# A gated mix of a 2-D spectral filter and a dense block: half of the tiles of x transposed by DMA

## The chip, the cores and the metric

The kernel runs on one core of one Trainium2 chip. The metric is the device time of one execution in microseconds (us). A core has a matrix engine (PE, with its weight loads PEld), a vector engine (DVE), an activation engine (ACT), a general engine (POOL) and a sync engine (SP) that issues DMAs; 16 DMA engines carry what SP, ACT and POOL issue.

## What is computed

```python
def _A_ref(x, w_r, w_i):                      # x: (1, 2048, 512)
    X = jnp.fft.rfft2(x.astype(jnp.float32))
    X = X * (w_r + 1j * w_i)                  # (2048, 257)
    return jnp.fft.irfft2(X, s=(S, D)).astype(jnp.bfloat16)

def _B_ref(x, w1, b1, w2):                    # w1: (512, 1792), w2: (1792, 512)
    h = jnp.einsum("bsd,df->bsf", x, w1) + b1
    sp = jnp.log1p(jnp.exp(-jnp.abs(h))) + jnp.where(h > 0, h, 0)
    return jnp.einsum("bsf,fd->bsd", h * jnp.tanh(sp), w2)

x = A_x
g = sigmoid((x * gate_w).sum(-1, keepdims=True))
return g * _A_ref(x, A_w_r, A_w_i) + (1 - g) * _B_ref(x, B_w1, B_b1, B_w2)
```

All inputs and the output are bfloat16. Both branches read the same x.

## The kernel before

The 2048 rows of x are 16 tiles of 128 rows by 512 columns; row 16 p + t of x is partition p of tile t, in `xo`. Both branches want x with its columns on the partitions, in `xT`. A tile gets there by four PE transposes of 128x128 into a PSUM bank (`tr{t}`, L522), which also sort the rows by an index `bx`, and one eviction by DVE or ACT (`evx{t}`, L451 or L452). All use bank 1, apart from tiles 1 to 3.

**Spectral branch.** It is a chain of small Fourier matrices. For each pair of tiles DVE makes four sums and differences (`ty`, `tz`, `t0`, `t2`, L537); for each tile PE does `a1` (L551 to L554, all in bank 0) and an eviction `e1` follows; for each four tiles PE does `s1` (L572, banks 2 to 5), four evictions `e2` bring it to `Ybuf`, and two DMAs `r1w` write it to `scr1`, a scratch in DRAM. When all of `scr1` is written, four DMAs `r1r` read it back in another order into `Abuf`. Then come four rounds of `s2` on PE (L689), the products with the filter W on DVE (L699), sums on POOL or DVE (L705), `s2i` (L732) and `r2w`, the trip through a second scratch, and at the end for each tile `s1i` (L764), `a1i` (L776), a scaling by the gate (L781) and two adds (L784).

**Dense branch.** Four chunks `c` of four tiles. `mm1` (L810) is 14 groups of four matmuls for a chunk, each followed by the activation on ACT (L819); `mm2` (L851) multiplies with w2 in two halves of seven matmuls for a tile. It has no latency of its own and stands between the steps of the spectral branch on PE.

**Gate.** `gdot` (L594, DVE) forms the dot products from `xo` once the third `s1` is placed; two small DMAs `gdj` on SP's queue sort them by `bx`; a sigmoid gives `gcol`.

**Order.** `_Graph.schedule` (L223) makes the order of every engine's work when the kernel is built. It takes the task that can start first by written-down durations, and among those within 0.1 us of it the one of the highest priority; a task of several possible engines goes where it ends first. For DMAs it keeps two clocks: `dq_free` for those issued by SP and ACT, `dq2_free` for POOL's, each with a written-down rate `bw` (POOL's with a factor 1.5). On the chip each engine then runs its list strictly in order and waits at an instruction until what it depends on is done.

**Loads.** SP's queue, in this order: x tile 0, tiles 1 to 3, w1 in pieces, the constants FD, tiles 4 to 7, M1's first half, w1, tiles 8 to 11, the last piece of w1 (`t_w1`), tiles 12 to 15, M1's second half, sm, gw, gd. POOL's queue: b1, then W in four DMAs and w2 in two, all of which wait for `t_w1`:

```python
        ld_x(8, 12)
        t_w1 = ld_w1(3)
        ld_x(12, 16)
        ...
                           writes=[("W", i, h)], nbytes=64 * 8224, queue="pool", deps=[t_w1])
```

W is first read by `wcols` on POOL (L609), whose result goes into two small matmuls `rcw` (L629, L630). All DMAs are issued at one line, L421.

Of the kernel before, what the change touches and what calls it, by code (L numbers as in the profile page):

```python
# [7 lines left out]
BF = mybir.dt.bfloat16  # L8
# [5 lines left out]
NT = 16  # L14
# [308 lines left out]
def _build(nc, A_x, A_w_r, A_w_i, B_x, B_w1, B_b1, B_w2, gate_w, out):  # L323
# [11 lines left out]
    with es:  # L335
        def sb(name, shape, dt):
            return es.enter_context(nc.sbuf_tensor(name, shape, dt))

        xo = sb("xo", [128, NT, 512], BF)
        xT = sb("xT", [128, 4, NT, 128], BF)  # L340
        Tg = sb("Tg", [128, 8192], BF)
        yb = sb("yb", [128, 2, 2, 256], BF)
        act = sb("act", [128, 3, NFT, 512], BF)
# [54 lines left out]
        psb = ps.bitcast(BF)  # L398

        xv = A_x[0].rearrange("(p t) d -> p t d", t=16)  # L400
        ov = out[0].rearrange("(a b t) d -> b a t d", b=2, t=16)
        w1v = B_w1.rearrange("(dt p) f -> p dt f", p=128)
        w2v = B_w2.rearrange("(ft p) n -> p ft n", p=128)
# [10 lines left out]
        out_sem = new_sem("s_out")  # L414
        n_out_dma = [0]

        def dma(name, dst, src, reads=(), writes=(), nbytes=0, deps=(), is_out=False, prio=None, queue="sp", bw=300e3):
            dur = 1.0 if queue == "pool" else 0.5

            def fn(e, _dst=dst, _src=src):  # L420
                return e.dma_start(_dst, _src)  # L421

            t = G.add(name, queue, dur, fn, reads=reads, writes=writes, lat=2.0 + nbytes / bw, deps=deps, prio=prio)
            t.xfer = nbytes / bw
            t.isdma = True
            if is_out:
                t.sem = out_sem
                n_out_dma[0] += 1
                t.semval = 16 * n_out_dma[0]
            else:  # L430
                t.sem = new_sem("d_" + name)
                t.semval = 16
            return t

        def mm(n):
            return n / 2400.0 + 0.0025
# [28 lines left out]
        def ld_x(t0, t1):  # L465
            dma(f"ld_x{t0}", xo[:, t0:t1, :], xv[:, t0:t1, :], writes=[("x", t) for t in range(t0, t1)], nbytes=128 * 1024 * (t1 - t0),
                bw=260e3 if t0 < 4 else 380e3)

        W1S = [(0, 2), (2, 6), (6, 10), (10, 14)]

        def ld_w1(i):
# [14 lines left out]
        ld_x(4, 8)  # L486
        ld_m1(0)
        ld_w1(2)
        ld_x(8, 12)
        t_w1 = ld_w1(3)  # L490
        ld_x(12, 16)
        ld_m1(1)
        dma("ld_sm", sm[:], d_SM[:], writes=["sm"], nbytes=128 * 1280)
        dma("ld_gw", gwb[:, :], gate_w.unsqueeze(0).to_broadcast([128, 512]), writes=["gw"], nbytes=128 * 1024)
# [1 line left out]
        for i in range(2):  # L496
            for h in range(2):
                dma(f"ld_W{i}{h}", WT[64 * h:64 * h + 64, i, :, :].rearrange("p g k -> p (g k)"), Wv[i][h],
                           writes=[("W", i, h)], nbytes=64 * 8224, queue="pool", deps=[t_w1])
        WALL = [("W", i, h) for i in range(2) for h in range(2)]  # L500
        for h in range(2):
            dma(f"ld_w2_{h}", w2_sb[:, 7 * h:7 * (h + 1), :], w2v[:, 7 * h:7 * (h + 1), :],
                writes=[("w2", h)], nbytes=128 * 7 * 1024, queue="pool", deps=[t_w1])


        G.add("zero", "dve", 0.15, lambda e: e.memset(zt[:, :], 0.0), writes=["zt"], prio=99.0)
# [7 lines left out]
        s1_tasks = []  # L514
        t_r1w = []
        for t in range(NT):
            tbk = 1 + t if 1 <= t < 4 else 1

            def f_tr(e, t=t, tbk=tbk):
                ins = None  # L520
                for dt_ in range(4):
                    ins = e.transpose(psb[:, tbk, 128 * dt_:128 * (dt_ + 1)], xo[:, t, 128 * dt_:128 * (dt_ + 1)], perm[:, :])  # L522
                return ins

            t_tr = pe(f"tr{t}", 4 * mm(128), f_tr, reads=[("x", t), "perm"], writes=[("bank", tbk)], prio=SP0 + 1.0)
            evict(f"evx{t}", 512, xT[:, :, t, :], psb[:, tbk, 0:512].rearrange("p (r j) -> p r j", r=4),
                  [("bank", tbk)], [("xT", t)], prio=SP0 + 1.0)
            if t == 3:
                pe("tr_small", 0.1, lambda e: e.transpose(psb[:, 0, 0:14], braw[0:14, :], id14[:, :]),
                   reads=["braw", "id14"], writes=[("bank", 0)], deps=[t_tr], prio=SP0 + 1.0)  # L530
                G.add("ev_small", "dve", 0.2, lambda e: e.tensor_copy(out=b1f[:, :], in_=psb[:, 0, 0:14]), reads=[("bank", 0)], writes=["b1f"], prio=SP0 + 1.0)

            if t % 2 == 1:
                t0, yi = t - 1, (t // 2) % 2

                def tt(name, o, i0, i1, op, n, reads, writes):
                    G.add(name, "dve", dve_dur(n, rate=2.0), lambda e: e.tensor_tensor(out=o, in0=i0, in1=i1, op=op),  # L537
                          reads=reads, writes=writes, prio=SP0 + 0.9)

                lo, hi = xT[:, 0:2, t0:t0 + 2, :], xT[:, 2:4, t0:t0 + 2, :]  # L540
                yy = yb[:, yi, :, :].rearrange("p r (t j) -> p r t j", t=2)
                xr = [("xT", t0), ("xT", t)]
                tt(f"ty{t}", yy, lo, hi, ALU.add, 512, xr, [("y", yi)])
                tt(f"tz{t}", Tb[:, 2:4, t0:t0 + 2, :], lo, hi, ALU.subtract, 512, xr, [("Tz", t0), ("Tz", t)])
                tt(f"t0{t}", Tb[:, 0, t0:t0 + 2, :], yy[:, 0], yy[:, 1], ALU.add, 256, [("y", yi)], [("T0", t0), ("T0", t)])
                tt(f"t2{t}", Tb[:, 1, t0:t0 + 2, :], yy[:, 0], yy[:, 1], ALU.subtract, 256, [("y", yi)], [("T2", t0), ("T2", t)])

        for t in range(NT):
            def f_a1(e, t=t):
                pr = ps[:, 0, :].rearrange("p (r x) -> p r x", r=4)  # L550
                e.matmul(pr[:, 0, :], Tb[:, 0, t, :], FDs[:, 0:128], start=True, stop=True)  # L551
                e.matmul(pr[:, 2, :], Tb[:, 1, t, :], FDs[:, 128:256], start=True, stop=True)
                for i in range(2):
                    ins = e.matmul(pr[:, 1::2, :], Tb[:, 2 + i, t, :], FDs[:, 256 + 256 * i:512 + 256 * i].rearrange("p (r x) -> p r x", r=2),  # L554
                                   start=(i == 0), stop=(i == 1))
                return ins

            pe(f"a1_{t}", 2 * mm(128) + 2 * mm(256), f_a1, reads=[("T0", t), ("T2", t), ("Tz", t), "FD"],
               writes=[("bank", 0)], prio=SP0)
            evict(f"e1_{t}", 512, In1[:, t, :].rearrange("p (c r q) -> p c r q", c=2, r=4),  # L560
                  ps[:, 0, :].rearrange("p (r c q) -> p c r q", r=4, c=2),
                  [("bank", 0)], [("In1", t)], prio=SP0 + 0.2)

            if t % 4 == 3:
                def f_s1(e, t0=t - 3):
                    ins = None
                    for tt_ in range(4):
                        tk = t0 + tt_
                        for c in range(2):
                            for bx in range(2):  # L570
                                r = slice(64 * bx, 64 * bx + 64)
                                ins = e.matmul(ps[:, 2 + 2 * (tt_ // 2) + bx, 256 * (tt_ % 2):256 * (tt_ % 2) + 256], M1s[r, tk, c, :],  # L572
                                               In1[r, tk, 256 * c:256 * c + 256], start=(c == 0), stop=(c == 1))
                    return ins

                B25 = [("bank", i) for i in range(2, 6)]
                s1_tasks.append(pe(f"s1_{t}", 8 * mm(256) + 0.19, f_s1, reads=[("In1", t - i) for i in range(4)] + [("m1", t // 8)], writes=B25, prio=SP0 + 0.4))
                for bx in range(2):
                    for i in range(2):
                        b0 = 16 * bx + t - 3 + 2 * i  # L580
                        evict(f"e2_{b0}", 512, Y1[:, b0:b0 + 2, :].rearrange("p b k -> p (b k)"), ps[:, 2 + 2 * i + bx, :],
                              [("bank", 2 + 2 * i + bx)], [("Y1", b0), ("Y1", b0 + 1)], prio=SP0 + 0.6)
            if t % 4 == 3:
                for bx in range(2):
                    b0 = 16 * bx + t - 3
                    t_r1w.append(dma(f"r1w{t}_{bx}", scr1_w[:, b0:b0 + 4, :], Y1[:, b0:b0 + 4, :],
                                     reads=[("Y1", b0 + i) for i in range(4)], writes=[("scr1", b0 + i) for i in range(4)],
                                     nbytes=128 * 4 * 512, prio=SP0 + 1.0))
# [211 lines left out]
        for c in range(NCH):  # L800
            hb = c % 3
            G.cur_prio = PR['mm1c0'] if c == 0 else PR['mm1c'] - c
            for ft in range(NFT):
# [3 lines left out]
                def f_mm1(e, c=c, ft=ft, bank=bank):  # L807
                    ins = None
                    for dt_ in range(4):
                        ins = e.matmul(ps[:, bank, :], w1_sb[:, dt_, 128 * ft:128 * (ft + 1)],  # L810
                                       xT[:, dt_, 4 * c:4 * c + 4, :], start=(dt_ == 0), stop=(dt_ == 3))
                    return ins

                t_mm1 = pe(f"mm1_{c}_{ft}", 4 * mm(512), f_mm1,
                   reads=[("xT", 4 * c + i) for i in range(4)] + [("w1", ft)], writes=[("bank", bank)])
                if c == 0 and ft == 0:
                    G.filled = t_mm1
                G.add(f"mish_{c}_{ft}", "act", act_dur(512, True),
# [162 lines left out]
```

## Time and profile before

| | us |
|---|---|
| median of 3 runs (lowest to highest) | 142.26 (142.17 to 143.02) |
| the profiled execution | 142.56 |
| its span, first to last instruction | 140.8 |
| PE busy | 136.2 |
| DVE busy | 86.3 |
| ACT busy | 81.4 |
| POOL busy | 31.9 |
| L522, the transposes: 64 matmuls, mean of one 0.242, busy | 6.7 |
| evictions of transposes: 10 on DVE of 0.424, 6 on ACT of 0.597 | |
| DMA moved 21.38 MB | |

Times inside an execution are counted from its first instruction. Busy time of PE is modelled and overlaps: a matmul of 512 columns shows 0.380 us, while in the chain of work four of them take 0.86 us. Of a DMA two things are shown: its issue on the queue of an engine, and the time from issue to landing; the packets of q1 are those of SP's queue, of q0 those of POOL's.

### The profile page before, as it was taken

To read this page: it belongs to the slowest core of one execution; us is meant where nothing else is said; L and a number is where in the kernel's file an instruction comes from. 1 tells how busy PE (TensorE), PEld (TensorE's weight loads), DVE (VectorE), ACT (ScalarE), POOL (GpSimd) and SP (SyncE) were. 2 spreads that over 40 slices of the span, in tenths; PEclk is the share of its full clock that TensorE was granted. 3 is DMA by queue.
4 is the path that set the end of the run, shared out by engine and by line. 5 is a ranking of instruction groups with operands and counts; after the bars stand their busy time and mean duration, and the time that the engine had idled before them with its cause. 6 is when DMAs were issued, how large, how long until landed. Compare 5 with 4: busy or idle time off the path is not lost.

```text
span 140.8 us, 2515 instructions
## 1 busy us (share of the span) xinstructions
PE 136.2 (97%) x946; PEld 74.2 (53%) x946; DVE 86.3 (61%) x192; ACT 81.4 (58%) x128; POOL 31.9 (23%) x62
## 2 busy tenths in 40 slices
PE   6999999999999999999999999999999999999991
PEld 4756656455544435435445444544444666766670
DVE  0276757748999303983983893592200499999831
ACT  4448797969874487488058437532411685776300
POOL 4000670003000001560440440340000144256400
PEclk9999999999999999999999999999999999999999
DMA  3999999999705485700300300300359615333422
GB/s 87 334 382 387 393 245 214 239 333 366 222 8 154 151 254 202 289 0 10 143 0 0 149 0 5 149 2 0 143 150 277 179 27 119 80 79 92 98 52 58
DMA packets 16556, 21.38 MB, mean 152 GB/s; under 512 B 1248, under 2 KB 12384, under 8 KB 16160
## 3 DMA queue, kind: packets, MB, share of 16 engines
q1 hardware_dynamic: 15552, 17.22, 39.3%
q0 software_dynamic: 832, 3.94, 10.4%
q8 instruction: 7, 0.11, 0.3%
q10 hardware_dynamic: 160, 0.07, 0.2%
q14 instruction: 5, 0.04, 0.1%
HBM read 14.92 MB, written 6.29 MB: 151 GB/s over the span
## 4 chain that ended last, share of the span: by engine, by line
PE 92%; ACT 4%; DVE 0%; issue 0%
PE ps L810 33%; PE ps L851 32%; PE ps L776 5%; PE ps L509 3%; PE ps L689 3%; PE ps L572 3%; PE ps L732 3%; PE ps L764 3%; PE ps L522 2%; ACT Ybuf L452 2%; PE ps L833 2%; PE ps L554 2%; ACT act L819 1%; PE ps L551 1%; ACT Abuf L452 1%; ACT xT L452 1%
## 5 line engine op out<-in xcount | busy, mean ns | idle before, releaser
L810 PE MATMUL ps<-xT,w_sb 128*128 128x512 bf16 x224 | 54.2, 380 | 0.4 <-ACT act L819 0.3
L819 ACT ACTIVATE act<-ps,b1f 128x512 bf16<-128x512 f32 x56 | 38.1, 690 | 21.8 <-PE ps L810 16.4
L851 PE MATMUL ps<-w_sb,act 128*128 128x512 bf16 x210 | 48.3, 379 | 0.0
L810 PEld LDWEIGHTS ps<-xT,w_sb 128*128 128x128 bf16 x224 | 20.0, 98 | 24.1 <-ACT act L819 5.7
L851 PEld LDWEIGHTS ps<-w_sb,act 128*128 128x128 bf16 x210 | 20.1, 98 | 22.4 <-issue 0.4
L699 DVE TENSOR_TENSOR misc<-ps,WT 128x512 f32<-128x512 f32 x32 | 19.9, 685 | 12.6 <-PE ps L689 12.6
L705 POOL TENSOR_TENSOR misc<-misc 128x255 bf16<-128x255 f32 x16 | 11.4, 731 | 41.0 <-DVE misc L699 41.0
L784 POOL TENSOR_TENSOR Tg<-misc 128x256 bf16<-128x256 f32 x12 | 10.3, 873 | 27.9 <-ACT misc L781 27.9
L790 ACT ACTIVATE xo<-ps,omg 128x512 bf16<-128x512 f32 x11 | 7.6, 687 | 15.2 <-PE ps L851 15.0
L451 DVE CAST Ybuf<-ps 128x512 bf16<-128x512 f32 (+1 forms) x10 | 8.8, 900 | 9.3 <-PE ps L732 8.2
L781 ACT ACTIVATE misc<-ps,gcol 128x512 f32<-128x512 f32 x16 | 10.3, 685 | 5.0 <-PE ps L776 4.0
L451 DVE CAST misc<-ps 128x512 bf16<-128x512 f32 x8 | 5.5, 683 | 11.4 <-PE ps L764 11.4
L784 DVE TENSOR_TENSOR Tg<-misc 128x256 bf16<-128x256 f32 x20 | 12.0, 629 | 0.7 <-ACT misc L781 0.7
L594 DVE SCALAR_TENSOR_TENSOR junk<-xo,gwb 128x512 bf16<-128x512 bf16 x16 | 11.0, 689 | 0.7
L452 ACT ACTIVATE Ybuf<-ps 128x512 bf16<-128x512 f32 (+1 forms) x14 | 9.4, 718 | 2.6 <-PE ps L572 1.6
L451 DVE COPY xT<-ps 128x512 bf16<-128x512 bf16 x10 | 4.2, 424 | 9.1 <-PE ps L522 9.0
L776 PE MATMUL ps<-GDs,misc 128*128 128x256 bf16 x64 | 9.3, 273 | 0.0
L452 ACT ACTIVATE Abuf<-ps 128x512 bf16<-128x512 f32 x12 | 7.2, 602 | 0.0
L776 PEld LDWEIGHTS ps<-GDs,misc 128*128 128x128 bf16 x64 | 6.0, 98 | 2.3
L522 PEld LDWEIGHTS ps<-pid,xo 128*128 128x128 bf16 x64 | 5.2, 110 | 3.0 <-issue 0.4
L522 PE MATMUL ps<-pid,xo 128*128 128x128 bf16 x64 | 6.7, 242 | 0.0
L705 DVE TENSOR_TENSOR misc<-misc 128x255 bf16<-128x255 f32 x16 | 6.4, 441 | 0.0
(81 smaller groups left out, 115.7 us busy)
## 6 DMA issues: line engine op xcount, KB each, us to landing
scr<-Ybuf SPq DMA_DIRECT2D x8, 256.0 KB, 9.3
Abuf<-scr SPq DMA_DIRECT2D x4, 512.0 KB, 4.5
scr<-Ybuf SPq DMA_DIRECT2D x4, 512.0 KB, 3.0
Abuf<-scr SPq DMA_DIRECT2D x8, 256.0 KB, 5.3
w_sb<-in_B_w_dram POOLq DMA_DIRECT2D x2, 896.0 KB, 17.5
out_dram<-xo SPq DMA_DIRECT2D x14, 128.0 KB, 2.3
w_sb<-in_B_w_dram SPq DMA_DIRECT2D x3, 512.0 KB, 7.9
xo<-in_A_x_dram SPq DMA_DIRECT2D x3, 512.0 KB, 8.7
```

The costliest lines, as they stand in the source:

```text
L451: G.add_multi(name, [("dve", dve_dur(n), lambda e: e.tensor_copy(out=dst, in_=src)), ("act", act_dur(n), lambda e: e.activation(dst, src, ...
L452: ("act", act_dur(n), lambda e: e.activation(dst, src, AF.Copy))],
L522: ins = e.transpose(psb[:, tbk, 128 * dt_:128 * (dt_ + 1)], xo[:, t, 128 * dt_:128 * (dt_ + 1)], perm[:, :])
L594: lambda e, t=t: e.scalar_tensor_tensor(out=junk[:, :], in0=xo[:, t, :], scalar=1.0, in1=gwb[:, :], op0=ALU.mult, op1=ALU.mult, accum_out= ...
L699: lambda e, Pb=Pb, Wu=Wu, bk=bk, pb=pb: e.tensor_tensor(out=Pb[:, pb, :].rearrange("p (c r q) -> p c r q", c=2, r=4), in0=ps[:, bk, :].rea ...
L705: fz = (lambda e, c=c, Pb=Pb, op=op, pb=pb, i=i, zb=zb: e.tensor_tensor(out=Zb[:, zb, i, c, 1:256], in0=Pb[:, pb, 1:256], in1=Pb[:, pb, 25 ...
L776: ins = e.matmul(ps[:, yk, 256 * (j // 2):256 * (j // 2) + 256], TT[:, ts_, j, :], GDs[:, j, :], start=(j % 2 == 0), stop=(j % 2 == 1))
L781: lambda e, t=t, gb=gb, yk=yk: e.activation(gEO[:, gb, :], ps[:, yk, :], AF.Copy, scale=gcol[:, t:t + 1]),
L784: fg = (lambda e, i=i, op=op, t=t, gb=gb: e.tensor_tensor(out=ga[:, t, 256 * i:256 * i + 256], in0=gEO[:, gb, 0:256], in1=gEO[:, gb, 256:5 ...
L810: ins = e.matmul(ps[:, bank, :], w1_sb[:, dt_, 128 * ft:128 * (ft + 1)], xT[:, dt_, 4 * c:4 * c + 4, :], start=(dt_ == 0), stop=(dt_ == 3))
L819: lambda e, ft=ft, bank=bank, hb=hb: e.activation(act[:, hb, ft, :], ps[:, bank, :], AF.Mish, bias=b1f[:, ft:ft + 1]),
L851: ins = e.matmul(ps[:, bank, :], act[:, hb, ft, 128 * tl:128 * (tl + 1)], w2_sb[:, ft, :], start=(ft == 0), stop=(ft == NFT - 1))
```

## The change

Tiles 8 to 15 of x are no longer transposed by PE. Four transposing DMAs (`ld_xt`, two for each four tiles, one for each `bx`) in SP's queue read them from DRAM into `xT` behind the last piece of w1. W and w2 no longer wait for `t_w1` but for the last of these (`t_xt`). Tiles 8 to 15 of x as they are, which `gdot` and the output still need in `xo`, are loaded by POOL's queue between W and w2. `xT` is laid out by tiles, so that a DMA's part of it is in one piece for each tile; `mm1` and the sums and differences read it through other strides. `a1` of tiles 8 to 15 uses banks 0 and 1 in turn. The rates for the new loads and w2 are written into the planner.

```diff
-        xT = sb("xT", [128, 4, NT, 128], BF)
+        xT = sb("xT", [128, NT, 4, 128], BF)
...
+        xtv = A_x[0].rearrange("(a b t) d -> b a (t d)", b=2, t=16)
...
-        def dma(name, dst, src, reads=(), writes=(), nbytes=0, deps=(), is_out=False, prio=None, queue="sp", bw=300e3):
+        def dma(name, dst, src, reads=(), writes=(), nbytes=0, deps=(), is_out=False, prio=None, queue="sp", bw=300e3, transpose=False):
...
-                return e.dma_start(_dst, _src)
+                return e.dma_start_transpose(_dst, _src) if transpose else e.dma_start(_dst, _src)
...
+        def ld_xt(g):
+            for bx in range(2):
+                t_ = dma(f"ld_xt{g}{bx}", xT[:, 4 * g:4 * g + 4, :, 64 * bx:64 * bx + 64].rearrange("p t r j -> p (t r) j"),
+                    xtv[bx, :, 2048 * g:2048 * g + 2048], writes=[("xT", t, bx) for t in range(4 * g, 4 * g + 4)], nbytes=128 * 2048,
+                    bw=150e3, transpose=True)
+            return t_
...
-        ld_x(8, 12)
-        t_w1 = ld_w1(3)
-        ld_x(12, 16)
+        ld_w1(3)
+        ld_xt(2)
+        t_xt = ld_xt(3)
...
-                           writes=[("W", i, h)], nbytes=64 * 8224, queue="pool", deps=[t_w1])
+                           writes=[("W", i, h)], nbytes=64 * 8224, queue="pool", deps=[t_xt])
...
+        for t0 in (8, 12):
+            dma(f"ld_x{t0}", xo[:, t0:t0 + 4, :], xv[:, t0:t0 + 4, :], writes=[("x", t) for t in range(t0, t0 + 4)], nbytes=128 * 4096,
+                queue="pool", deps=[t_xt], bw=500e3)
...
-                writes=[("w2", h)], nbytes=128 * 7 * 1024, queue="pool", deps=[t_w1])
+                writes=[("w2", h)], nbytes=128 * 7 * 1024, queue="pool", deps=[t_xt], bw=500e3)
...
-            tbk = 1 + t if 1 <= t < 4 else 1
+            if t < 8:
+                tbk = 1 + t if 1 <= t < 4 else 1
...
-                lo, hi = xT[:, 0:2, t0:t0 + 2, :], xT[:, 2:4, t0:t0 + 2, :]
+                lo, hi = [xT[:, t0:t0 + 2, i:i + 2, :].rearrange("p t r j -> p r t j") for i in (0, 2)]
...
-            def f_a1(e, t=t):
-                pr = ps[:, 0, :].rearrange("p (r x) -> p r x", r=4)
+            a1b = t % 2 if t >= 8 else 0
+
+            def f_a1(e, t=t, a1b=a1b):
+                pr = ps[:, a1b, :].rearrange("p (r x) -> p r x", r=4)
...
-                                       xT[:, dt_, 4 * c:4 * c + 4, :], start=(dt_ == 0), stop=(dt_ == 3))
+                                       xT[:, 4 * c:4 * c + 4, dt_, :], start=(dt_ == 0), stop=(dt_ == 3))
```

More of the change, by code (lines that the diff above doesn't have):

```diff
@@ L516, in _build, with f_tr @@
         for t in range(NT):
-            tbk = 1 + t if 1 <= t < 4 else 1
[L519 to L527, printed above, removed]
+            if t < 8:
+                tbk = 1 + t if 1 <= t < 4 else 1
+                def f_tr(e, t=t, tbk=tbk):
+                    ins = None
+                    for dt_ in range(4):
+                        ins = e.transpose(psb[:, tbk, 128 * dt_:128 * (dt_ + 1)], xo[:, t, 128 * dt_:128 * (dt_ + 1)], perm[:, :])
+                    return ins
+                t_tr = pe(f"tr{t}", 4 * mm(128), f_tr, reads=[("x", t), "perm"], writes=[("bank", tbk)], prio=SP0 + 1.0)
+                evict(f"evx{t}", 512, xT[:, t, :, :], psb[:, tbk, 0:512].rearrange("p (r j) -> p r j", r=4),
+                      [("bank", tbk)], [("xT", t, bx) for bx in range(2)], prio=SP0 + 1.0)
             if t == 3:
@@ L538, in tt @@
                           reads=reads, writes=writes, prio=SP0 + 0.9)
-                lo, hi = xT[:, 0:2, t0:t0 + 2, :], xT[:, 2:4, t0:t0 + 2, :]
+                lo, hi = [xT[:, t0:t0 + 2, i:i + 2, :].rearrange("p t r j -> p r t j") for i in (0, 2)]
                 yy = yb[:, yi, :, :].rearrange("p r (t j) -> p r t j", t=2)
-                xr = [("xT", t0), ("xT", t)]
+                xr = [("xT", t0 + i, bx) for i in range(2) for bx in range(2)]
                 tt(f"ty{t}", yy, lo, hi, ALU.add, 512, xr, [("y", yi)])
@@ L558, in _build @@
             pe(f"a1_{t}", 2 * mm(128) + 2 * mm(256), f_a1, reads=[("T0", t), ("T2", t), ("Tz", t), "FD"],
-               writes=[("bank", 0)], prio=SP0)
+               writes=[("bank", a1b)], prio=SP0)
             evict(f"e1_{t}", 512, In1[:, t, :].rearrange("p (c r q) -> p c r q", c=2, r=4),
-                  ps[:, 0, :].rearrange("p (r c q) -> p c r q", r=4, c=2),
-                  [("bank", 0)], [("In1", t)], prio=SP0 + 0.2)
+                  ps[:, a1b, :].rearrange("p (r c q) -> p c r q", r=4, c=2),
+                  [("bank", a1b)], [("In1", t)], prio=SP0 + 0.2)
             if t % 4 == 3:
@@ L810, in f_mm1 @@
                         ins = e.matmul(ps[:, bank, :], w1_sb[:, dt_, 128 * ft:128 * (ft + 1)],
-                                       xT[:, dt_, 4 * c:4 * c + 4, :], start=(dt_ == 0), stop=(dt_ == 3))
+                                       xT[:, 4 * c:4 * c + 4, dt_, :], start=(dt_ == 0), stop=(dt_ == 3))
                     return ins
                 t_mm1 = pe(f"mm1_{c}_{ft}", 4 * mm(512), f_mm1,
-                   reads=[("xT", 4 * c + i) for i in range(4)] + [("w1", ft)], writes=[("bank", bank)])
+                   reads=[("xT", 4 * c + i, bx) for i in range(4) for bx in range(2)] + [("w1", ft)], writes=[("bank", bank)])
                 if c == 0 and ft == 0:
```

## The prediction

> **What bounds the kernel now.** I read the totals and the chain first, then the chain in order of time, then the DMA queues stretch by stretch. From the profile's page:
>
> ```profile
> PE 136.2 (97%) x946; PEld 74.2 (53%) x946; DVE 86.3 (61%) x192; ACT 81.4 (58%) x128; POOL 31.9 (23%) x62
> PE 92%; ACT 4%; DVE 0%; issue 0%
> L522 PE MATMUL ps<-pid,xo 128*128 128x128 bf16 x64 | 6.7, 242 | 0.0
> ```
>
> PE sets the time: 92% of the chain, and its queue never stands empty long. So an instruction taken from PE is worth its issue time, and a wait put in front of PE costs its whole length. The transposes are L522. Now the chain in order of time (start us, us, what):
>
> ```profile
> 13.19 0.22 PE ps L522 x4
> ...
> 14.83 1.00 PE ps L572 x16
> ...
> 23.41 1.00 PE ps L572 x16
> ...
> 31.13 0.98 PE ps L572 x16
> ...
> 40.44 0.98 PE ps L572 x16
> ...
> 53.98 0.99 PE ps L689 x16
> ```
>
> One tile's four transposes are 0.22 us of chain. L572 is s1, once per four tiles; L689 is the first s2. Between the last s1 and the first s2 lie 13.5 us in which the spectral path goes out to scr1 and comes back (r1w, r1r), and PE works on the dense branch. PE's order is fixed at build time: it runs s2 where `schedule` put it, whether the data are there or not. Next the POOL queue in order of time, where W and w2 are issued:
>
> ```profile
> 15.32 1.12 POOL L421 DMA_DIRECT2D WT<-in_A_w_r_dram  x2 [12.46 <-DMA w_sb<-in_B_w_dram]
> ...
> 31.93 0.19 POOL L609 COPY wrv<-WT 128x2 bf16<-128x2 bf16 x1 [10.52 <-DMA WT<-in_A_w_i_dram]
> ```
>
> W is issued when the last piece of w1 has landed, and is all there 16.6 us later. The DMA queues in 18 to 27 us (queue: packets, MB, share of 16 engines), and in 36 to 40 us below it:
>
> ```profile
> q0 software_dynamic: 276, 1.87, 93.6%
> q1 hardware_dynamic: 193, 0.15, 10.0%
> ```
> ```profile
> q1 hardware_dynamic: 1049, 0.52, 44.5%
> ```
>
> q0 is POOL's queue, q1 SP's. While W runs, q0 holds the engines with packets of 6.8 KB, and q1, with packets of about 0.5 KB for scr1, moves 0.15 MB in 9 us. Alone, a packet of q1 costs 44.5% x 64 us / 1049 = 27 ns, which is 0.30 MB per us. What that does to r1w, issue to landing, for those issued in 16 to 18 us, and for the last two, issued at 42.3 and 42.9 us:
>
> ```profile
> DMA to landing us min/median/max: 17.5/18.5/19.4
> ```
> ```profile
> DMA to landing us min/median/max: 2.3/2.5/2.6
> ```
>
> The same 256 KB take 18.5 us beside W and w2 and 2.5 us without. Before the change this is free: w2 has landed at about 36.7 us (issued 18.4, longest 18.3), the late r1w have caught up by 40.1 (34.0 + 6.1), and only then, at 42.3, does the last r1w start.
>
> **What is removed.** Eight tiles of transposes: 8 x 0.22 = 1.8 us off PE. Their eight evictions (0.42 us on DVE, 0.60 on ACT) go too. PE's idle time in 15 to 32 us, where ACT held it up, is 10.00 - 9.94 + 7.00 - 6.72 = 0.34 us; I take 0.3 of gain (0 to 0.34). That is -2.1 us, if nothing else happens. The new layout of xT I cost at nothing: mm1 then reads four pieces of 128 columns, and L732, which reads pieces of 64, takes 0.98 us per 16 as L572 does with whole rows. The DVE adds keep runs of 128 elements. If that failed, each of 224 mm1 matmuls would pay.
>
> **The transposes' own time** is in no row. w1's last piece lands earlier, since tiles 8 to 11 (0.52 MB) no longer stand in front of it: at 0.39 MB per us (0.78, 0.74 and 0.81 MB in the three stretches of 2 us from 10 on) that is 1.35 us, so 15.3 - 1.35 = 14.0. Lower bound for 1.05 MB: the same rate, 2.7 us. Upper bound: they land in runs of 128 bytes, 8192 of them over 16 engines at 27 ns, 13.9 us. The source pieces under one transposed block are 256 bytes wide: 4096 / 16 x 27 ns = 7.0 us. I take 7.0, since a packet of 512 bytes is the nearest row. Tiles 8 to 11 are then there at 17.5, 12 to 15 at 21.0.
>
> The Trainium skill, DMA: Bandwidth & Descriptors, section Latency and other measured facts, puts a transposing DMA at 261 GB/s with a non-contiguous middle dimension. By that the 1.05 MB take an estimated 4.0 us and the sum below falls by 3.0 us; no row of this profile shows a transpose. Its section Rules for kernel authors says that a transpose next to ordinary DMAs needs nothing, which speaks against the wait: by it W could go at 14.0.
>
> Issuing: SP's DMAs take 0.43 to 0.51 us each, and SP stands idle from 9.9 to 17.0 us, so four transposes cost nothing up to 1.8 us each. Behind them in SP's queue are M1's second half, sm, gw and gd (1.08 MB, 2.8 us: there at 23.8) and r1w of tiles 0 to 3. M1 is wanted by the third s1, which I put at 27 below.
>
> **What the wait moves.** W and w2 go at 21.0 instead of 15.3, and tiles 8 to 15 of x now stand between them. Behind the waiting DMA on POOL are the rr copies and wcols; nothing needs them before 36. Before, W and w2 took 36.7 - 15.3 = 21.4 us. After it SP's loads hold them up 1.3 us less (0.52 MB less), and x adds 1.05 MB at 0.34 MB per us, 3.1 us: 23.2 us, so q0 is done at 44.2. W alone is there at 21.0 + 15.3 = 36.3. x is there at 39.4, and gdot of tile 8 may hold DVE 3 us; w2 lands with the first mm2, which ran at 43.3. Each of these can hold PE 1 to 3 us, but all lie inside the next wait, so I add nothing for them.
>
> **The new wait.** `schedule` counts SP's and POOL's transfers on two clocks of their own (dq_free, dq2_free), so its order knows nothing of the starving. In that order tiles 8 to 15 go fast: no transposes, and a1 has two banks. a1 of tiles 1 to 3 came every 1.42 us with a transpose and an mm1 between; without the transpose 1.2. So the second s1 is at about 21, the third at 27, the last at 33 instead of 40.4. The order's round trip is the trace's: last s1 to s2 13.5 us, less 2.4 us for the gdj DMAs that stood between the r1r (47.2 to 48.5, with their wait), which now come later: s2 at about 45 (41 to 46).
>
> The data come otherwise. r1w is 2.1 MB. While q0 runs it moves what it moved before: 0.15 MB in 9 us of W, 0.18 MB in the 5 us from 27 to 32, so some 0.7 MB by 44.2, with the engines that finish early. The other 1.4 MB take 4.7 us, landing at 49. The first two r1r then land and s2 starts 5 us on (first at 45.55 took 3.8, the next 4.2): 54, as late as before. PE stands from 45 to 54: +9.0 us. The work that before covered the trip has been done ahead of it.
>
> **Sum.** The profiled execution took 142.56 us (span 140.8 and 1.76 around it), 0.30 above the median. 142.56 - 1.8 - 0.3 + 9.0 = 149.46; against the median 149.2. With transposes in 2.7 us and s2 at 46 the wait is 49.7 - 46 = 3.7 and the time 143.9; with s2 at 41 and 7.0 it is 13, 153.2. The likeliest case's own range is 143.9 to 153.2.
>
> **Rivals.** *The trip is covered (faster, 17%).* If the order puts s2 at 54 or later, or the starving is milder because x's packets (4 KB) share the engines more evenly, only the gain is left: 142.26 - 2.1 = 140.2, with half a microsecond for the tail, down to 139.6. The place is the first s2; it decides from the point where r1w's backlog drains before PE gets there. For it: 97% PE, and 28 mm1 of later chunks as cover. Against it: 18.5 us of landing in the same surroundings.
>
> *W alone is late (within 1%, 14%).* wcols and its small matmuls rcw wait for W at 36.3 + 1.2, and the order may want them 2 us earlier; if s2 is late in the order, this is the only stall: 140.2 + 2 = 142.2. For it: W's 16.6 us; against it: rcw before ran only after the last s1, at 44.8.
>
> *The transposes crawl (slower, 9%).* At 13.9 us or more, tiles 8 to 11 come at 21 and all of q0 7 us later: s2 at 61, 149.2 + 7 = 156.2. The DMA might also be split into elements, which would be far beyond this. For it: packets under 512 bytes have no row here. Against it: whole rows of 4 KB in the source.
>
> **Numbers.** Forecast 60%. 1% is about what a measurement of this kernel can tell from no change. Faster by over 1% is the first rival, 0.17; within it the second, 0.14; slower 0.60 + 0.09 = 0.69. The range, 139.6 to 155.0, takes in both better cases and leaves out the crawl.
>
> **What would show it.** Right: L522 at 32, the last s1 near 33, r1w issued in 17 to 35 us landing after 10 us or more, a PE gap before L689 with the r1r as releaser, q0 busy until about 44. Wrong: L689 starts without a gap, or well before 50; r1w lands in a few microseconds; or PE stands earlier, at a1 of tile 8, which would make it the transposes.

## The result, and the profile after

The changed kernel takes 151.22 us (median of 4 runs, 150.09 to 151.61) against 142.21 for the kernel before: ratio 1.061, 95% interval 1.054 to 1.068. The profiled execution took 151.61 us with a span of 149.9, that is 9.1 more than the span before. Ratios are formed from the faster of a kernel's executions alone; in e3, e4, e8 and e9 some were slower, in the first three the profiled one too, so there the median of all lies above the ratio, and the profile is read for what waits for what, not for its total.

The chain by engine, and the granted clock in 40 slices of the span, from the page of the changed kernel:

```profile
PE 64%; DMA 21%; SPq 10%; POOL 2%; issue 1%; DVE 0%; POOLq 0%
...
PEclk9999999999999556999999999999999999999999
```

The chain no longer lies on PE alone: a third of it runs over DMAs and SP's queue. The clock falls in three slices, which it never did before. The chain in order of time shows the place (start us, us, what):

```profile
22.27 13.90 DMA WT<-in_A_w_i_dram
...
38.04 3.46 PE ps L824 x16
41.50 6.15 DMA scr<-Ybuf
...
48.12 6.00 DMA Abuf<-scr
54.11 0.14 issue
54.25 1.92 PE ps L703 x16
56.17 3.32 PE ps L824 x8
```

L703 is the first `s2` (L689 before), L824 `mm1`. The last r1w starts at 41.5 us and lands 6.15 later; then the r1r; then s2 at 54.25. Before, s2 stood at 53.98. So the spectral path is no earlier, though its last `s1` is. The waits say how long PE stood (engine line, waited for: total, times, longest):

```profile
PE ps L703 <- DMA Abuf<-scr: 8.0, 1, 8.0
...
PE ps L643 <- POOL wh L625: 0.9, 1, 0.9
```

And the three later `s1` in order of time, which came early, as the order wanted:

```profile
22.07 1.05 PE L586 MATMUL ps<-Abuf,m1g 64*128 64x256 bf16 x16
...
27.06 1.05 PE L586 MATMUL ps<-Abuf,m1g 64*128 64x256 bf16 x16
...
32.26 1.05 PE L586 MATMUL ps<-Abuf,m1g 64*128 64x256 bf16 x16
```

The last is 8.2 us earlier than before (40.44), and all of that is given back. From issue to landing, the two r1w issued at 24.3 and 24.8 us took (their mean is the median shown):

```profile
DMA to landing us min/median/max: 17.6/18.8/20.0
```

The difference of the spans adds up: transposes -1.8 (32 matmuls less of 0.055 us), wait at the first s2 +8.0, wait at rcw +0.9, the low clock +2.4 (the first s2 takes 1.92 us instead of 0.99, the next eight mm1 3.32 instead of the 1.83 that eight take later in the same chain), and -0.3 for PE's idle time in 15 to 32 us (0.07 instead of 0.34): +9.2, of the 9.1 measured.

### The profile page after: what moved, and what is told of

It reads as the page before. It is cut to its first block, busy times and chain, and to the rows that moved or that the text cites. A ratio compares the mean times of both kernels' runs of the same rounds, so it can differ in the third digit from the quotient of the medians.

```text
span 149.9 us, 2451 instructions
## 1 busy us (share of the span) xinstructions
PE 136.3 (91%) x914; PEld 72.2 (48%) x914; DVE 86.5 (58%) x188; ACT 79.2 (53%) x123; POOL 33.8 (23%) x65
## 4 chain that ended last, share of the span: by engine, by line
PE 64%; DMA 21%; SPq 10%; POOL 2%; issue 1%; DVE 0%; POOLq 0%
PE ps L865 30%; PE ps L824 18%; SPq L422 10%; DMA WT<-in_A_w_i_dram 9%; PE ps L790 5%; DMA scr<-Ybuf 4%; DMA Abuf<-scr 4%; PE ps L703 3%; DMA xT<-in_A_x_dram 3%; PE ps L746 3%; PE ps L778 2%; PE ps L847 2%; POOL WT L422 1%; POOL wrv L623 0%; POOL wrv L624 0%
## 5 line engine op out<-in xcount | busy, mean ns | idle before, releaser
L824 PE MATMUL ps<-xT,w_sb 128*128 128x512 bf16 x224 | 55.0, 388 | 0.1
L824 PEld LDWEIGHTS ps<-xT,w_sb 128*128 128x128 bf16 x224 | 20.1, 99 | 26.7 <-ACT act L833 6.6
L798 DVE TENSOR_TENSOR Tg<-misc 128x256 bf16<-128x256 f32 x20 | 13.3, 703 | 1.1 <-ACT misc L795 1.1
L703 PE MATMUL ps<-Abuf,sm 128*64 128x256 bf16 x64 | 5.1, 312 | 8.0 <-DMA Abuf<-scr 8.0
L703 PEld LDWEIGHTS ps<-Abuf,sm 128*64 128x64 bf16 x64 | 3.9, 124 | 9.7 <-issue 8.5
L452 DVE COPY xT<-ps 128x512 bf16<-128x512 bf16 x5 | 2.1, 425 | 7.1 <-PE ps L534 7.1
L453 ACT ACTIVATE Abuf<-ps 128x512 bf16<-128x512 f32 x10 | 5.9, 595 | 0.0
```

Source lines behind the costliest of these rows:

```text
L452: G.add_multi(name, [("dve", dve_dur(n), lambda e: e.tensor_copy(out=dst, in_=src)), ("act", act_dur(n), lambda e: e.activation(dst, src, ...
L453: ("act", act_dur(n), lambda e: e.activation(dst, src, AF.Copy))],
L703: ins = e.matmul(ps[64 * h:64 * h + 64, SB[i], 256 * c:256 * c + 256], RF[:, c, :], In2[:, 16 * h + u0 + i, :], start=True, stop=True)
L798: fg = (lambda e, i=i, op=op, t=t, gb=gb: e.tensor_tensor(out=ga[:, t, 256 * i:256 * i + 256], in0=gEO[:, gb, 0:256], in1=gEO[:, gb, 256:5 ...
```

## The experiments

Theory S: r1w starves (gets few turns at the DMA engines) behind POOL's queue, which the wait for the transposes pushed back, while the order fixed at build time brings PE to the first s2 early and with nothing to do in the gap. Rival T: the transposing DMAs cost the time themselves. Further rivals stand with each.

**e1, the order alone.** One number of the planner; the transfers stay what they are.

```diff
+                    if t.name.startswith("r1w"):
+                        t.done = max(t.done, dq2_free + 5.0)
```

> Every transfer is as in the changed kernel; only the planner's number for r1w is changed (landed not before POOL's queue is through, plus 5 us), so PE, DVE and ACT get another order, with the first s2 behind more dense work. Theory S (r1w starves behind POOL's queue, and the fixed order has nothing in the gap): r1w still lands at about 47.6 us and the first s2 still starts at 54 to 55, but the gap of 8.0 us before it falls under 1.5 and PE's clock stays at 1.0; 140 to 143 us. Rival T (the transposes themselves cost the time, by coming late or by what they hold up): the order of s2 doesn't matter, 149 to 152.

Measured: 142.91 us, ratio to before 1.0032 (1.0010 to 1.0055), clock 1.0. Around the first s2 (L705) its chain has no gap:

```profile
54.18 1.73 PE ps L826 x8
55.91 0.99 PE ps L705 x16
```

So nearly all of the loss is the uncovered trip, and T falls as its reason: the same four transposing DMAs are in this kernel, POOL goes on at 20.03 us instead of 20.65, and 8.3 us of the loss are gone. That they cost nothing at all is not shown (see e9 and e10). And the 1.8 us did not come out. PE still waits in two places, and s2 stands 1.9 us later than before:

```profile
PE ps L645 <- POOL wh L627: 1.0, 1, 1.0
PE ps L792 <- ACT misc L455: 1.0, 1, 1.0
```

The first is rcw, waiting for W; the second is an `a1i` near the end. The two are 2.0 of the 2.7 us that are missing from the 140.2 us that the gain would give. That the late spectral path causes the second wait is argued, not shown.

**e2, W and the rest don't wait.** Every engine's order is that of the changed kernel.

```diff
-        ld_w1(3)
+        t_w1 = ld_w1(3)
...
         order = G.schedule()
+        for t in G.tasks:
+            if t.isdma and t.eng == "pool":
+                t.deps = [t_w1 if d is t_xt else d for d in t.deps]
```

> Same order on every engine as in the changed kernel, but POOL's six large loads and two x loads wait for the last piece of w1 and not for the transposes. Theory S says that an engine takes packets from two queues in turn whatever their size: the transposes' small packets then starve behind W, x and w2 as r1w did (one per 474 ns of W), land near 35 to 38 us instead of 20, and PE stands before a1 of tiles 8 to 15 for 12 us or more: 153 to 165 us. Rival P (a transpose next to ordinary DMAs needs nothing): transposes land before 24, POOL's queue drains 6 us earlier, s2 starts at 48 to 49, 144 to 147 us.

Measured: 157.66 us, ratio 1.110 (1.105 to 1.115). W goes at 14.2 us, the last transpose lands at 36.9, and DVE stands 15.4 us for it, PE 14.7:

```profile
DVE yb L549 <- DMA xT<-in_A_x_dram: 15.4, 1, 15.4
...
PE ps L565 <- DVE Tg L549: 14.7, 1, 14.7
```

Its DMA queues in 16 to 26 us (queue: packets, MB, share of 16 engines):

```profile
q0 software_dynamic: 288, 1.97, 91.0%
q1 hardware_dynamic: 973, 0.24, 18.3%
```

Beside POOL's queue the transposes move 0.24 MB in 10 us; in the changed kernel, where they go before it, all 1.05 MB took some 7 us. My reason was one packet of theirs for each of W; it is 3.4 (973 to 288), and still far too few. In this order the wait in the change is needed, then. The Trainium skill (DMA: Bandwidth & Descriptors, section Rules for kernel authors) says that a transpose next to ordinary DMAs needs nothing; the row that says so is about corrupted values and promises nothing on the time, for which this run decides.

**e3, w2 out of the way.** The order of the changed kernel, but w2 stands behind wcols on POOL and waits for the second r1r.

```diff
         order = G.schedule()
+        p = order["pool"]
+        late = [t for t in p if t.name.startswith("ld_w2")]
+        for t in late:
+            p.remove(t)
+            t.deps = [t_r1r[1]]
+        i = [t.name for t in p].index("wcols") + 1
+        p[i:i] = late
```

> Same order as in the changed kernel but for w2: its two DMAs stand behind wcols on POOL and wait until the second r1r has landed. Theory S: POOL's queue is through by 36 to 37 us instead of 44, r1w lands at 41 to 43 instead of 47.6, the first s2 starts at 47 to 49 instead of 54.2 (gap 0.5 to 2.5 us); w2 lands at about 52 to 54 and may hold the first mm2 by 1 to 3 us: 144 to 147.5 us. Rival T: s2 moves by less than 2 us, 149 to 152.

Measured: 150.54 us, ratio 1.047 (1.041 to 1.052). The waits of PE moved as one stretch of its instructions shows (start us, us, engine line op, idle before and releaser):

```profile
48.87 1.06 PE L703 MATMUL ps<-Abuf,sm 128*64 128x256 bf16 x16 [2.31 <-DMA Abuf<-scr]
...
61.62 3.17 PE L865 MATMUL ps<-w_sb,act 128*128 128x512 bf16 x7 [3.28 <-DMA w_sb<-in_B_w_dram]
```

The mechanism is as expected: with 1.8 MB less in POOL's queue the r1r go at 42.6 instead of 47.7 and s2 starts 5.4 us earlier. The total was missed. In the profiled execution w2 landed at 61.6 and not at 52 to 54: it was issued at 49 and 50 and took 11.5 us, beside the rest of the r1r and 1 MB of constants (`c_g`). The bytes in the way of the trip have to be moved at some time, and w2 was soon wanted.

**e4, the clock.** Before the first s2, PE waits for the other engines' work that s2 needs, does 64 matmuls on zeros, and then waits for the DMAs; transfers and order stay.

```diff
...
+                    for _ in range(64):
+                        eobj.matmul(ps[:, 3, 0:256], zt[:, 0:128], zt[:, :], start=True, stop=True)
```

> Same transfers and order; in front of the first s2, once its banks are free, PE does 64 matmuls of 256 columns on zeros, whose results are written over: about 6.9 us of the gap of 8.0. If the low granted clock after the gap (0.50 to 0.61 in 48 to 60 us) comes from PE's standing still, it stays at 1.0, the first s2 takes 0.98 us instead of 1.92, and 2.0 to 2.6 us are won: 148.3 to 149.4 us. If the clock fell for another reason, 150.5 to 151.8 us. The start of the first s2 (54.2) stays in both.

Measured: 149.15 us, ratio 1.045 (1.040 to 1.051), clock 1.0 throughout. The first s2, in its chain:

```profile
55.19 1.06 PE ps L703 x16
```

It took 1.06 us instead of 1.92, though it began at 55.19 and not, as expected, at 54.2 (the second r1r took 6.98 us instead of 6.00). Against the changed kernel's ratio of 1.061 that is 1.6%, some 2.2 us, near the 2.4 us read from the trace. The low clock is a consequence of standing still, and it is no cause of the gap.

**e5, the wait alone.** The kernel before in its own order, all tiles transposed by PE; W and w2 wait for the last load in SP's queue.

```diff
-        dma("ld_gd", GDs[:], d_GD[:], ...)
+        t_gd = dma("ld_gd", GDs[:], d_GD[:], ...)
...
         order = G.schedule()
+        for t in G.tasks:
+            if t.isdma and t.eng == "pool":
+                t.deps = [t_gd if d is t_w1 else d for d in t.deps]
```

> The kernel before in its own order, all sixteen tiles transposed by PE, but W and w2 wait for the last load in SP's queue (gd, at about 19.5 us) instead of the last piece of w1 (15.3). Theory S: POOL's queue is through 4 to 5 us later, near 41, and r1w of tiles 0 to 11 catches up near 44; the last r1w is issued at 42.3 as before and lands at 46 to 48 instead of 45.5, so the first s2 (53.98) starts 0.5 to 2.5 us later: 142.5 to 144.8 us. So the late start of W alone costs little where the last s1 is late too. Rival (the late start of W and w2 alone makes the loss, by rcw, the filter products or the first mm2): 146 us or more.

Measured: 142.31 us, ratio 0.9989 (0.9973 to 1.0004). W went at 21.1 us, later than in the change, and cost nothing. From issue to landing, the r1w of tiles 4 to 7 (issued at 26), and below them the last two (at 42.5 and 43.1):

```profile
DMA to landing us min/median/max: 14.2/14.3/14.4
```
```profile
DMA to landing us min/median/max: 2.3/2.5/2.6
```

I had expected 0.5 to 2.5 us; the backlog was gone when the last r1w started. POOL's queue, which has no x in this kernel, was through but for 0.03 MB at 38 us; what one as late as the changed kernel's (43) would cost in the order before is not shown. What harms the changed kernel is an early last s1 together with a late POOL queue: e1 takes away the one, e3 the other.

**e7 and e9, no transposing.** Order and waits of the changed kernel; the four transposing DMAs become plain copies of as many bytes.

```diff
-                t_ = dma(f"ld_xt{g}{bx}", xT[:, 4 * g:4 * g + 4, :, 64 * bx:64 * bx + 64].rearrange("p t r j -> p (t r) j"),
-                    xtv[bx, :, 2048 * g:2048 * g + 2048], ..., transpose=True)
+                t_ = dma(f"ld_xt{g}{bx}", xT[64 * bx:64 * bx + 64, 4 * g:4 * g + 4, :, :].rearrange("p t r j -> p (t r) j"),   # e7
+                    xv[64 * bx:64 * bx + 64, 8:16, :].rearrange("p t (r j) -> p (t r) j", r=4)[:, g - 2::2, :], ...)
...
+                t_ = dma(f"ld_xt{g}{bx}", xT[64 * bx:64 * bx + 64, 4 * g:4 * g + 4, :, :].rearrange("p t r j -> p t (r j)"),   # e9
+                    xv[64 * bx:64 * bx + 64, 4 * g:4 * g + 4, :], ...)
```

> Order and waits of the changed kernel; the four transposing DMAs are replaced by four plain ones that copy as many bytes into xT in pieces of 256 bytes without transposing, so tiles 8 to 15 do not have the reference's values. Theory S (the price is the queue's time and what it pushes back, not the transposing): the copies land at 18 to 21 us (20.4 with transposes), the first s2 starts at 52 to 54.5, 148.5 to 151.5 us. Rival X (transposing as such holds up the DMA engines): the copies land before 16.5, s2 before 50.5, under 147.5 us.

> As e7_copy256, but in pieces of 4 KB (tiles 8 to 15 do not have the reference's values): the 1.05 MB at the rate of ordinary loads, 2.7 us. Theory S: POOL goes on at 16.5 to 17 us, its queue is through 4 us earlier, the first s2 starts at 49.5 to 51 instead of 54.2, gap 3 to 5 us: 145 to 147.5 us, so still slower than before, though these tiles' transposes cost next to nothing. Rival T (the transposes' time is the loss): no gap over 1 us, 140 to 142.5 us.

Measured: e7 150.39 us, ratio 1.057 (1.053 to 1.061); e9 148.69, ratio 1.044 (1.041 to 1.047). In e7 POOL goes on at 20.50 us, in the changed kernel at 20.65, and the first s2 starts at 53.27 instead of 54.25: transposing as such (rival X) is not what holds POOL up. e9 was expected at 145 to 147.5, with POOL going on at 17. It went on at 19.54: these copies run at 0.25 MB per us (0.48 and 0.50 MB in the two stretches of 2 us from 14 on), not at 0.39 as the ordinary loads. The line of W's arrival in the changed kernel, the same in e9, and e9's first s2:

```profile
36.31 0.44 POOL L623 COPY wrv<-WT 128x2 bf16<-128x2 bf16 x1 [9.77 <-DMA WT<-in_A_w_i_dram]
```
```profile
33.05 0.20 POOL L623 COPY wrv<-WT 128x2 bf16<-128x2 bf16 x1 [7.61 <-DMA WT<-in_A_w_i_dram]
...
51.72 1.92 PE L703 MATMUL ps<-Abuf,sm 128*64 128x256 bf16 x16 [6.62 <-DMA Abuf<-scr]
```

s2 comes 2.5 us earlier than in the changed kernel, after a wait of 6.6, and the time is 2.5 us less. POOL's earlier issue accounts for 1.1 of the 3.3 us by which W is there earlier. For the rest the trace points to SP's queue: SP is done with the copies at 9.2 us, with the transposes only at 17.8, and so M1's second half, sm, gw and gd go out by 11.5 instead of 19.8. In the changed kernel these and the first r1w hold the DMA engines from 20 to 24 us (1.12 MB, 97.2% of the engines), and no packet of POOL's queue moves before 24.2, 3.6 us after its first issue; in e9 the first moves at 21.5, 2.0 us after. With neither is the loss gone.

**e8, w2 late and the planner told.** e7's copies, and both cures together: w2 waits for the last r1w, and the planner gets later times for r1w, r1r and w2.

```diff
+                    if t.name.startswith("r1r"):
+                        t.done += 3.0
+                    if t.name.startswith("r1w"):
+                        t.done = max(t.done, dq2_free + 4.5)
...
-                writes=[("w2", h)], nbytes=128 * 7 * 1024, queue="pool", deps=[t_xt], bw=500e3)
+                writes=[("w2", h)], nbytes=128 * 7 * 1024, queue="pool", deps=[t_xt], bw=300e3)
...
+        for t in G.tasks:
+            if t.name.startswith("ld_w2"):
+                t.deps.append(t_r1w[-1])
```

> e6_best with the copies of e7_copy256 in place of the transposes (tiles 8 to 15 do not have the reference's values): w2 waits for the last r1w, the planner is told when r1w, r1r and w2 land. Theory S: the last r1w lands at 41 to 43, the first s2 starts at 49.5 to 52 with no gap over 1 us before it, w2's halves land at 48 to 54, PE's clock stays at 1.0: 140.2 to 142.2 us. Rival U (what the DMAs carry beside the trip sets the first s2 or the first mm2): a gap of 2 us or more before one of them, 143 to 146 us.

The text on record speaks of e6_best: that is this kernel with the transposing DMAs, for which there is no result. Measured: 144.32 us, ratio 1.012 (1.010 to 1.015), in the range of rival U. In the profiled execution PE waits before w2's first use, and for W:

```profile
PE ps L869 <- DMA w_sb<-in_B_w_dram: 2.5, 1, 2.5
...
PE ps L647 <- POOL wh L629: 1.3, 1, 1.3
```

The order had put a part of `mm2` (L869) in front of the first s2. w2, issued at 42.8 beside 2 MB of r1r, landed at 53.8; s2 came at 56.5.

**e10, both limits kept.** e9's copies with e1's change (plus 3 us instead of 5).

> e9_copy4k (tiles 8 to 15 copied untransposed in pieces of 4 KB, so without the reference's values) with e1_order's one change: the planner is told that r1w lands no earlier than POOL's queue is through plus 3 us. Theory S with its corollary (the 1.8 us come out only if the first s2 stands covered and is not later than before): r1w lands at 45 to 46, the first s2 starts at 52 to 53.5 without a gap over 1 us, before it at most 1 us at rcw: 140.3 to 141.9 us. Rival V (the spectral chain from the last s1 on is not the second limit; e1_order lost its gain to something else): 142.3 us or more, with the same tail as e1_order.

Measured: 140.35 us, ratio 0.9858 (0.9841 to 0.9874), clock 1.0. In its chain rcw (L645) and the first s2 (L705):

```profile
37.55 0.03 PE ps L645
...
53.06 0.99 PE ps L705 x16
```

There is no wait at either, s2 is 0.9 us earlier than before and 2.9 earlier than in e1, and the whole gain of 2.0 us is there. The kernel leaves out the transposing of tiles 8 to 15, so it can't be used, but it shows that e1 did not lose the work taken off PE. Against e1 two things differ, the loads and the planner's number, and the runs do not part them. What the trace shows of the loads: W is there at 33.4 us instead of 35.9, though issued only 0.2 us earlier (19.8, 20.0); SP has sent M1's second half and the loads behind it by 11.6, much as in e9. No run with the transposing DMAs is faster than the kernel before.

## Why the prediction was right

The result (151.22 for 149.2 forecast) came by the mechanism that was named. By its steps:

| step | predicted | measured |
|---|---|---|
| work taken off PE | 1.8 us | 32 matmuls, 1.8 |
| PE's idle time in 15 to 32 us won | 0.3 | 0.27 |
| transposes over, W issued | 21.0 | 20.65 |
| W all there | 36.3 | 36.31 |
| second, third, last s1 | 21, 27, 33 | 22.07, 27.06, 32.26 |
| PE reaches the first s2 | 45 | 46.26 |
| POOL's queue through | 44.2 | 43, but for 0.03 MB |
| r1w still to move then | 1.4 MB | 0.8 MB at 44 |
| last r1w landed | 49 | 47.65 |
| from there to the first s2 | 5 | 6.6 |
| first s2 starts | 54 | 54.25 |
| PE stands | 9.0 | 8.0, and 0.9 at rcw |

The wait at rcw had been put inside the next wait, and it was: without it PE would have come to s2 at 45.4 and stood 8.9. That s2 started at the forecast time is in part luck: less of r1w was left than estimated, so it landed 1.3 us early, and the r1r took 1.6 us longer. What the sum lacked is the clock, +2.4 us, and this is nearly the whole difference between forecast and result. It could not be seen in the kernel before, where PE never stood still for long.

The price taken for the transposes, 27 ns for a packet of 256 bytes, gave 7.0 us, and the time came out right, but not for that reason. In 14 to 16 us 1617 of their packets took 93.9% of the 16 engines' 2 us, 18.6 ns each; at that price all 4096 would take an estimated 4.8 us. The rest is pauses. GB/s in 14 to 16 us, in 40 equal slices, of the changed kernel, and below it of e7:

```profile
GB/s 15 20 15 56 251 271 297 287 292 292 282 297 237 283 282 297 282 292 292 282 297 276 77 210 282 297 282 297 287 297 282 282 391 15 20 0 10 31 36 5
```
```profile
GB/s 190 195 149 159 138 169 174 195 210 195 225 169 220 184 200 185 179 169 174 154 205 169 174 143 148 200 215 174 230 256 241 205 251 215 241 200 215 205 205 210
```

The transposes move mostly 250 to 300 GB/s and stop; e7's plain copies in pieces of 256 bytes run at about 193 without a stop, at 26.8 ns a packet by the same measure (1530 in 128.1%, since packets overlap). So the 27 ns fit plain copies of this size; that the transposes, cheaper by the packet but with pauses, let POOL go on at the same time is luck. Why they pause is not shown. The figure weighed against it, 261 GB/s or an estimated 4.0 us by the Trainium skill (DMA: Bandwidth & Descriptors, section Latency and other measured facts), is near what they move while they flow, but as the price of the whole it would have been too low here: in 14 to 18 us, pauses included, the queue moved 0.66 MB, 165 GB/s.

One step was badly off: issuing the four transposes was put at 0.5 us each, free up to 1.8. From the timeline of SP's queue, a warning in the kernel before, an ordinary load of x in the same place, and the transposes in the changed kernel:

```profile
5.83 1.95 SPq L421 DMA_DIRECT2D xo<-in_A_x_dram  x1
```
```profile
5.42 12.37 SPq L422 DMA_TRANSPOSE xT<-in_A_x_dram  x4
```

It took 12.4 us in all, 3.1 each. M1's second half was issued at 17.8 instead of 7.8. PE did not wait for it at the third s1 (27.06), but W did, as far as the traces show: it was there 15.7 us after its issue, and 13.5 and 13.6 in e9 and e10, where SP was free early. The sum did not miss this, because it took W's time from the kernel before, where W stood behind SP's loads too (16.6 us).

Of the rivals, the covered trip is what e1 built by hand, and it gave no gain by itself (142.91). The late W alone is e5's reading: no price in the order before; in the new orders PE waits at rcw 0.9 to 1.3 us in the changed kernel, e1, e3, e4, e7 and e8, and not in e9 and e10. The crawl did not occur.

## What to carry to other kernels

Where an order is fixed at build time, an earlier step is worth nothing, or worse, if the planner doesn't know what its transfers will meet: ask what else is in the DMA engines when the early step's DMAs are issued, and give the planner that time. Ask also what stands behind the early step's DMAs in the queue that issues them. A small-packet transfer beside a large-packet queue is to be priced by the end of that queue, not by its own bytes. And work taken off the bounding engine comes out only if the second limit, here the spectral path from its last s1 to its first s2, does not become later at the same time: e1 covered the trip and came out at 142.91, e10, with W 2.4 and s2 2.9 us earlier, at 140.35.

## What the runs showed of the hardware

In and after 8 us without work (46.26 to 54.25) PE's granted clock was 0.61 in 48 to 52 us, 0.50 in 52 to 56 and 0.61 in 56 to 60, although PE was at work again from 54.25; busy work in the gap held it at 1.0 (e4). These lines are from the table of stretches of the changed kernel (us, then PE, PEld, DVE, ACT and POOL busy with counts, granted clock, DMA share, GB/s):

```profile
48.00:52.00 4.00, 0.00 (x0) 0.00 (x0) 0.00 (x0) 0.00 (x0) 0.00 (x0) 0.61 0.72 190
52.00:56.00 4.00, 1.75 (x16) 1.48 (x16) 0.00 (x0) 0.00 (x0) 0.00 (x0) 0.50 0.90 334
56.00:60.00 4.00, 4.00 (x24) 1.49 (x23) 3.32 (x7) 1.96 (x2) 1.41 (x2) 0.61 0.54 179
```

The transposing DMAs beside W got 3.4 small packets for each large one and moved 24 GB/s (e2); before W they moved 250 to 300 GB/s between pauses, and their four issues held SP's queue for 12.4 us (the changed kernel). Plain copies into 64 partitions in pieces of 4 KB ran at 0.25 MB per us (e9), where the kernel before loaded into 128 partitions at 0.37 to 0.41 (0.74 to 0.81 MB in 2 us).
